# Pairing half slots with full ones in a routed expert layer behind block attention

## The chip, the core and the metric

The kernel runs on one core of a Trainium2 chip. The metric is the device time of one execution in microseconds. Below, PE is TensorE (matmuls and transposes), PEld its weight loads, DVE is VectorE, ACT is ScalarE, POOL is GpSimd and SP is SyncE, which here issues most of the transfers. A line number such as L764 is a line of the kernel before.

## The reference

Attention over 4 batches, 8 heads, 768 positions and 64 dimensions: every query sees the keys less than 16 positions away and one summary key and value for each block of 32 positions (the maximum of the keys, the mean of the values). Its output, 3072 tokens of 512 numbers, goes through a layer of 8 experts of which each token uses one.

```python
k_sum = k.reshape(B, H, nb, block, D).max(axis=3)
v_sum = v.reshape(B, H, nb, block, D).mean(axis=3)
mask_l = np.abs(pos[:, None] - pos[None, :]) < window
scores_s = scale * np.einsum('bhsd,bhnd->bhsn', q, k_sum) + np.log(block)
a = softmax(concatenate([where(mask_l, scores_l, -1e9), scores_s]))
x = matmul(a, concatenate([v, v_sum]))            # then 3072 x 512
e_idx = np.argmax(x @ w_gate, axis=1)
eom = 1.0 / (1.0 + np.exp(-(x @ w_output_gate)))
for e in range(E):
    mask = e_idx == e
    h = np.maximum(x[mask] @ w1[e], 0.0)          # w1: 512 x 1024
    ye = h @ w2[e]                                # w2: 1024 x 512
    out[mask] = gate_w[mask, None] * eom[mask, e, None] * ye
```

With the inputs as drawn, the reference assigns 17, 172, 596, 1384, 768, 0, 135 and 0 tokens to the eight experts; of the first two batches' 1536 tokens, 172, 596 and 768 go to experts 1, 2 and 4.

## The kernel before

**Attention** (`attention`) goes through 48 stages: 4 batches, 6 tiles of 128 positions in each, 2 groups of 4 heads in each tile. A stage makes scores (L321), masks them and takes their minimum on VectorE (L329), exponentiates on ScalarE (L331), transposes (L339), multiplies with the values (L350) and normalises (L358 to L360). Keys and queries are loaded raw, reordered (`reorder`, L205) and transposed (`prep_k`, `prep_q`). `k_sum` copies the block maxima of the keys into the key tile. The block means of the values come from `v_sum`: in batch 0 four sums on VectorE (L230), later adds on GpSimd (L237, L241); `mean` scales them and sends them to DRAM, from where `load_vsum` fetches them into the value windows beside those that `load_vw` brings. The issue order of SyncE in attention is the order in which the code is written; that of the other engines is set by a planner that orders the instructions by its own estimate of times.

**Routing** (`route`) finds each token's expert and its place in the expert's list, and writes token number and gate into the list `l_dr` with one scatter for each tile of 128 tokens (L448, GpSimd). x itself is written to `x_dr` (L363).

**Experts** work in slots. A full slot holds 256 tokens of one expert, a half slot 128. For a slot GpSimd fetches its list (`fetch_list`, L699) and gathers its rows (`fetch`, L712); `take_x` transposes them; `first` makes the hidden layer tile by tile (L763 to L767) and `second` the output (L852 to L854); `write` scales it and scatters it to the output (L872 to L877). Every weight is split into two parts, so each product takes three matmuls, and each tile of raw weights costs a conversion on ScalarE and one on VectorE (L733, L734). `fetch_w` loads the next slot's weights into rings of raw buffers: six before the second pool is open and for w1, ten for w2 after that. While a slot is computed, the rows of the next are transposed at tile 4 of `second`, and the rows of the one after it are gathered.

Slots 0 and 1 are "early": their lists hold tokens of which the list places are known when the routing of the first two batches is done, and slot 0 is started among the last batch's work (`late_work`, `early`). `early_slots` and `rest_slots` compute on VectorE which rows of the lists and which expert each slot has (`slot_tables`). After the early ones come SURE = 6 full slots that are run for any counts, and then, each within a branch on counts that were computed on the chip, more full slots (`more_full`, L903) and then half slots (`more_half`, L910). Each branch is nested in the body of the one before. For the tokens above, 12 full slots and 3 half slots are run. In a half slot the product is made the other way round (L807 to L809) and turned (L820).

The steps of the prediction touch L224 to L247, L293 to L296, L363, L448, L511 to L513, L557, `slot_tables` (L569), `rest_slots` (L633), and in `Experts` `fetch_list`, `fetch`, `first`, `full`, `start`, `early`, `half`, `second`, `write`, `run`, `rest`, `more_full` and `more_half`.

## Time and profile before

| | |
|---|---|
| median of 3 runs | 565.68 us (562.95 to 571.04) |
| the profiled execution | 563.66 us |
| its span, first to last instruction | 561.8 us |
| granted TensorE clock, mean | 0.949 |
| PE busy | 500.7 us (89%) |
| DVE busy | 395.9 us (70%) |
| ACT busy | 339.1 us (60%) |
| POOL busy | 193.1 us (34%) |
| read from HBM, written | 105.50 MB, 13.79 MB |

All times inside the execution count from its first instruction. In the page's slices the span is cut into 40 equal parts of 14 us, and each digit is a busy share in tenths; PEclk is the granted clock in tenths. A row of the timeline gives start, length, engine, line, operation, output and inputs, the count of merged instructions, and in brackets how long the engine had stood idle before it and what ended that. A row of the waits gives who waited for whom, the total, the count and the longest.

### The profile page before, as it was taken

The page shows a single profiled execution, that of the slowest core. Times are in us where ns is not written, and L with a number is a line of the kernel's source. Part 1 is how long each engine was busy: PE and PEld are TensorE (multiplying, and loading weights), DVE is VectorE, ACT ScalarE, POOL GpSimd, SP SyncE. Part 2 cuts the span into 40 slices and gives each one's busy share as a digit, 9 for nine tenths or more (in the row PEclk, how much of TensorE's full clock was granted, in tenths as well). Part 3 has the DMA queues.
Part 4 walks back from the last instruction along what each step waited for, and adds up shares of the span by engine and source line. Part 5 has one row for each costly group of instructions (what it writes and reads, how often), then busy time and mean ns, then how long its engine had stood idle before and what let it go on. Part 6 is the DMA issues. An engine that isn't in the chain of part 4 may idle for free. (4 is left out here: it accounts for less than half of the span.)

```text
span 561.8 us, 12246 instructions
## 1 busy us (share of the span) xinstructions
PE 500.7 (89%) x3880; PEld 436.5 (78%) x3880; DVE 395.9 (70%) x1210; ACT 339.1 (60%) x752; POOL 193.1 (34%) x222
## 2 busy tenths in 40 slices
PE   6498998988979789985999999999999999987990
PEld 5497786767768678874989989899898998975770
DVE  8878798759838857952767665776656666666892
ACT  4386786675749747442656554665555655547881
POOL 6036145445541420337643625415113031130111
PEclk8599998998979979997999999999999999998996
DMA  9979999999764874159667485774856737439790
GB/s 233 232 186 251 235 241 250 115 219 232 163 138 120 247 253 150 65 162 317 211 225 272 151 282 185 236 277 139 300 181 232 269 128 264 168 114 332 252 322 26
DMA packets 116799, 117.63 MB, mean 209 GB/s; under 512 B 53598, under 2 KB 78462, under 8 KB 115952
## 3 DMA queue, kind: packets, MB, share of 16 engines
q1 hardware_dynamic: 107584, 97.02, 61.3%
q0 software_dynamic: 9136, 19.69, 11.5%
q8 instruction: 34, 0.56, 0.5%
q14 instruction: 45, 0.37, 0.2%
HBM read 105.50 MB, written 13.79 MB: 212 GB/s over the span
## 5 line engine op out<-in xcount | busy, mean ns | idle before, releaser
L764 PE MATMUL hp<-xhl,w1h 128*128 128x256 f32 x384 | 109.0, 285 | 0.0
L765 PE MATMUL hp<-xhl,w1l 128*128 128x256 f32 x384 | 108.8, 284 | 0.0
L763 PE MATMUL hp<-xhl,w1h 128*128 128x256 f32 x384 | 108.4, 286 | 0.0
L733 ACT ACTIVATE w2h<-raw 128x512 fp32r<-128x512 f32 x104 | 64.7, 629 | 60.5 <-PE yp L854 27.7
L734 DVE TENSOR_TENSOR w2l<-raw,w2h 128x512 fp32r<-128x512 f32 x104 | 70.5, 689 | 35.2 <-ACT w2h L733 34.2
L852 PE MATMUL yp<-w2h,hh 128*128 128x512 f32 x216 | 87.3, 404 | 0.1
L853 PE MATMUL yp<-w2l,hh 128*128 128x512 f32 x216 | 85.4, 395 | 0.0
L854 PE MATMUL yp<-w2h,hl 128*128 128x512 f32 x216 | 85.2, 396 | 0.1
L331 ACT ACTIVATE pr<-sm,mn 128x120 f32<-128x120 f32 x192 | 62.1, 387 | 26.1 <-DVE mn L329 25.8
L763 PEld LDWEIGHTS hp<-xhl,w1h 128*128 128x128 f32 x384 | 73.7, 193 | 2.0 <-DVE w1l L734 0.4
L712 POOL DMA_INDIRECT xg<-x_dr,lst x28 | 32.3, 1152 | 124.5 <-PE xp L745 106.1
L764 PEld LDWEIGHTS hp<-xhl,w1h 128*128 128x128 f32 x384 | 74.1, 193 | 1.2 <-DVE xhl L748 0.2
L765 PEld LDWEIGHTS hp<-xhl,w1l 128*128 128x128 f32 x384 | 74.1, 193 | 0.0
L766 ACT ACTIVATE hh<-hp 128x256 fp32r<-128x256 f32 x96 | 36.5, 381 | 59.1 <-PE hp L765 57.0
L734 DVE TENSOR_TENSOR w1l<-raw,w1h 128x512 fp32r<-128x512 f32 x104 | 66.2, 690 | 7.3 <-ACT w1h L733 6.2
L767 DVE SCALAR_TENSOR_TENSOR hl<-hp,hh 128x256 fp32r<-128x256 f32 x96 | 39.6, 421 | 44.8 <-ACT hh L766 44.7
L321 PE MATMUL sp<-kt,qt 128*128 128x120 f32 x384 | 58.7, 301 | 7.9 <-DVE kt L296 7.0
L733 ACT ACTIVATE w1h<-raw 128x512 fp32r<-128x512 f32 x104 | 58.2, 621 | 6.9 <-DMA raw<-in_moe_w_dram 6.5
L321 PEld LDWEIGHTS sp<-kt,qt 128*128 128x128 f32 x384 | 53.8, 215 | 10.4 <-issue 8.3
L329 DVE CUSTOM_DVE_ANT_0 sm<-sp,c_sb 128x120 f32<-128x120 f32 x192 | 42.9, 277 | 14.6 <-PE sp L321 13.1
L854 PEld LDWEIGHTS yp<-w2h,hl 128*128 128x128 f32 x216 | 40.7, 189 | 9.5 <-DVE hl L823 0.5
L852 PEld LDWEIGHTS yp<-w2h,hh 128*128 128x128 f32 x216 | 41.2, 191 | 8.6 <-ACT hh L822 0.5
(285 smaller groups left out, 906.5 us busy)
## 6 DMA issues: line engine op xcount, KB each, us to landing
raw<-in_moe_w_dram SPq DMA_DIRECT2D x208, 256.0 KB
vw<-in_v_dram SPq DMA_DIRECT2D x88, 96.0 KB
raw_k<-in_k_dram SPq DMA_DIRECT2D x12, 512.0 KB
raw_q<-in_q_dram SPq DMA_DIRECT2D x12, 512.0 KB
vm<-in_v_dram SPq DMA_DIRECT2D x8, 768.0 KB
x_dr<-xs POOLq DMA_DIRECT2D x24, 256.0 KB, 5.8
vw<-vs_dr SPq DMA_DIRECT2D x36, 48.0 KB
vw<-in_v_dram SPq DMA_DIRECT2D x8, 64.0 KB
```

The lines of the kernel that those rows point to most:

```text
L321: nc.tensor.matmul(sp[:, 2 * x + y, 0:W], lhsT=qt[:, 2 * g + x, li, :], rhs=kt[:, 2 * g + x, blk * KW:blk * KW + W], start=True, stop=True)
L329: nc.vector.tensor_tensor_reduce(out=sm[:, c, :], in0=sp[:, c, 0:W], in1=c_sb[:, m:m + W], scale=1.0, scalar=3.0e38, op0=ALU.add, op1=ALU. ...
L331: nc.scalar.activation(pr[:, c, :], sm[:, c, :], AF.Exp, bias=mn[:, c:c + 1], scale=-1.0)
L733: nc.scalar.activation(hi, raw, AF.Copy)
L734: nc.vector.tensor_tensor(lo, raw, hi.bitcast(F32), ALU.subtract)
L763: nc.tensor.matmul(hp, lhsT=w_h[:, fs], rhs=self.xh[:, c, :], start=c == 0, stop=False)
L764: nc.tensor.matmul(hp, lhsT=w_h[:, fs], rhs=self.xl[:, c, :], start=False, stop=False)
L765: nc.tensor.matmul(hp, lhsT=w_l[:, fs], rhs=self.xh[:, c, :], start=False, stop=c == NC - 1)
L767: nc.vector.scalar_tensor_tensor(hl[:, j, :], hp, 0.0, hh[:, j, :].bitcast(F32), ALU.max, ALU.subtract)
L852: nc.tensor.matmul(y, lhsT=hh[:, j, tk], rhs=w_h, start=j == 0, stop=False)
L853: nc.tensor.matmul(y, lhsT=hh[:, j, tk], rhs=w_l, start=False, stop=False)
L854: nc.tensor.matmul(y, lhsT=hl[:, j, tk], rhs=w_h, start=False, stop=j == NF - 1)
```

## The change

1. Half slots are run in pairs with full ones: `more` runs a full slot and then a half slot in the body of one branch, as often as both are there, and the next pair is nested in it. What is left over, full slots or half slots, stands in the else branch of the pair that is not run, and full and half leftovers are the two arms of a further branch. The last full slots that are left over have a form of their own, `left`: the second product is made for one half of the tokens and written, then for the other half, whose scaling is split over VectorE and ScalarE.
2. The early slots are three, from the lists of the first two batches; "routed" comes in the third batch, and the gather of an early slot is bounded to those two batches' rows. SURE is 5.
3. Scatters of list entries are kept pending. Each write of a tile of x issues two of them; those of the last batch are issued two each behind the ReLU of tiles 1, 4 and 7 of `first` in the next slots. They have a bounds check.
4. Slot 0's weight tiles (8 of w1, 4 of w2) are loaded one by one, three in each of the last batch's tiles 0 to 3, and its list and rows in tiles 1 and 2; before, they came in tiles 3 and 4.
5. The tables of the slots are computed after slot 0's `second` rather than ahead of it, in three parts (sure, pairs, leftovers) beside the early one, and the lists are fetched two a slot.
6. At the start, the sums over v of batch 0 stay on VectorE for four heads only, behind the last copy of `k_sum`; those of the other four heads go to GpSimd, and the means to ScalarE and GpSimd. The reorder of q comes one tile after its load.

```diff
@@ constants
-EARLY = 2
-REST = N - EARLY * SLOT
-SURE = -(-(REST - E * SLOT // 2) // SLOT)
-MOST = (REST + E * (SLOT // 2 - 1)) // SLOT
-NITEM = MOST + 2
+EARLY = 3
+FIRST = 2
+SURE = -(-(N - EARLY * SLOT - E * SLOT // 2) // SLOT)
+MOST = (N + E * (SLOT // 2 - 1)) // SLOT
+PAIRS = max(min((N - h + (E - h) * (SLOT // 2 - 1)) // SLOT - SURE, h) for h in range(E + 1))
+NWOV = SURE + 2 * PAIRS + 2
+NLEFT = max(MOST - SURE, E) + 2
+NITEM = NWOV + NLEFT
@@ body
                     moe.open_first(tc.tile_pool(name="moe1", bufs=2, side="left", reuse_waits="tile"))
+                    moe.start(late_work)
                 elif event == "routed":
                     moe.add_slots(early_slots(tc, const, c_sb, rt))
-                    moe.start(late_work)
                 elif event[0] == "tiles done":
-                    moe.early(event[1])
+                    with tc.manual_schedule(engines={mybir.EngineType.Pool}):
+                        moe.early(event[1])
...
-                slots, halves, counts = rest_slots(tc, const, c_sb, rt)
-            moe.add_slots(slots)
-            moe.fetch_list(EARLY, 2)
-            moe.fetch_w(1, 1, range(NF // 2, NF))
-            moe.second(0, 2, *moe.hidden0, 1, 2, 2)
-            halves = halves()
-            moe.run(halves)
+            moe.fetch_w(1, ("e", 1), range(NF // 2, NF))
+            moe.second(("e", 0), 2, *moe.hidden0, ("e", 1), ("e", 2), 2, 2)
+            counts = rest_slots(tc, const, c_sb, rt, moe)
+            moe.run()
@@ v_sum, mean
-        if b == 0:
+        if (b, o) == (0, 0):
...
+            tc.add_manual_dep(i.ins, km["last"].name, mybir.DependencyInfo(mybir.DependencyClass.NoSync,
+                                                                           mybir.DependencyReason.SCHED_ONLY))
...
-        nc.vector.tensor_scalar(r2, total, 1.0 / 32.0, None, ALU.mult)
+        if b == 0 and o == 0:
+            nc.scalar.activation(r2, total, AF.Copy, scale=1.0 / 32.0)
+        else:
+            (nc.gpsimd if b == 0 else nc.vector).tensor_scalar(r2, total, 1.0 / 32.0, None, ALU.mult)
@@ values
-            nc.gpsimd.dma_start(x_dr[n0:n0 + P, :], xs.rearrange("p h d -> p (h d)"))
+            i = nc.gpsimd.dma_start(x_dr[n0:n0 + P, :], xs.rearrange("p h d -> p (h d)"))
+            scatter(tc, rt, 2, i.ins)
@@ attention, per tile
             if n2 and tt == 0:
                 load("q", q, *n2)
+            elif n2:
                 reorder("q", *n2, RE[5])
...
-        if b == B - 1 and i == n - 2 * TB + 5:
+        if i == n - 2 * TB - 3:
             yield "routed"
+def scatter(tc, rt, n, after, sync=False):
+    for _ in range(min(n, len(rt["pending"]))):
+        i = rt["pending"].pop(0)()
...
+        tc.add_manual_dep(i.ins, after.name, info)
+        rt["scatters"].append(i.ins)
@@ Experts
-            for sc in self.rt["scatters"]:
+            for sc in self.rt["scatters"][:FIRST * TB if s[0] == "e" else None]:
...
-    def full(self, s, nxt, nxt2):
+    def full(self, s, nxt, nxt2, nxt_n=2, lists=()):
         hidden = self.hidden()
         for j in range(NF):
-            self.first(j, hidden, nxt, "S" if j % 2 else "PT")
-        self.second(s, 2, *hidden, nxt, nxt2, 2)
+            i = self.first(j, hidden, nxt, "S" if j % 2 else "PT")
+            if j % 3 == 1:
+                scatter(self.tc, self.rt, 2, i, True)
+        for x in lists[:1]:
+            self.fetch_list(x, 2)
+        self.second(s, 2, *hidden, nxt, nxt2, nxt_n, 2, lists[1:])
+    def left(self, x, lists=()):
...
+        for t in range(2):
+            for j in range(NF):
+                if t == 0 and j == 4:
+                    self.take_x(2)
+                    self.fetch(nxt2, 2)
+                self.second_block(j, yp, hh, hl, [t])
+            self.write(s, yp, [t], t == 1)
@@ start
-        for s in range(EARLY):
-            self.fetch_list(s, 2)
-        self.fetch(0, 2)
-        late_work[3] += [lambda: self.fetch_w(1, 0, range(NF))]
-        late_work[4] += [lambda: self.fetch_w(2, 0, range(NF // 2))]
+        late_work[1] += [lambda: self.fetch_list(("e", 0), 2)]
+        late_work[2] += [lambda: self.fetch(("e", 0), 2)]
+        late_work[3] += [lambda: self.fetch_list(("e", 1), 2)]
+        parts = [(1, i) for i in range(NF)] + [(2, i) for i in range(NF // 2)]
+        for x, (which, i) in enumerate(parts):
+            late_work[x * 4 // len(parts)].append(lambda which=which, i=i: self.fetch_w(which, ("e", 0), [i]))
@@ write
+            if both:
+                h = DM // 2
+                nc.vector.tensor_scalar(y[:, 0:h], yp[t][:, 0:h], lst.bitcast(F32)[:, t, 1:2], None, ALU.mult)
+                nc.scalar.activation(y[:, h:], yp[t][:, h:], AF.Copy, scale=lst.bitcast(F32)[:, t, 1:2])
+            elif t == 0:
@@ in place of the loop over more_full and more_half
+    def more(self, k, n_pairs, n_full, n_half):
+        seen = dict(self.expert)
+        pair = None
+        if k < PAIRS:
+            with self.tc.If(n_pairs > k) as pair:
+                x = SURE + 2 * k
+                lists = [("w", y) for y in range(x + 3, min(x + 5, NWOV))]
+                self.full(("w", x), ("w", x + 1), ("w", x + 2), 1, lists[:1])
+                for y in lists[1:]:
+                    self.fetch_list(y, 2)
+                self.half(("w", x + 1), ("w", x + 2), ("w", x + 3), 2)
+                self.more(k + 1, n_pairs, n_full, n_half)
+            self.expert = dict(seen)
+        with pair.Else() if pair else contextlib.nullcontext():
+            with self.tc.If(n_full > 0) as left:
+                self.left_full(0)
+                self.more_full(1, MOST - SURE - k, n_full)
+            self.expert = dict(seen)
+            with left.Else():
+                self.more_half(0, E - k, n_half)
+        self.expert = seen
```

The slots are named by their kind and place: "e" early, "w" sure and paired, "l" left over.

229 lines of the change are left out of this document (149 added, 80 removed).

## The prediction

> **What bounds the kernel now.** I read the page's slices first, then the busy time by stage, then the order of TensorE's work at the seams between slots, and last the waits and the branches.
>
> ```profile
> PE   6498998988979789985999999999999999987990
> PEclk8599998998979979997999999999999999998996
> GB/s 233 232 186 251 235 241 250 115 219 232 163 138 120 247 253 150 65 162 317 211 225 272 151 282 185 236 277 139 300 181 232 269 128 264 168 114 332 252 322 26
> ```
>
> The busy time by stage:
>
> ```profile
> 150.00:185.00 35.00, 30.34 (x344) 26.54 (x339) 22.11 (x133) 24.46 (x65) 10.28 (x14) 0.90 0.64 149
> 260.00:400.00 140.00, 140.00 (x904) 127.12 (x903) 91.28 (x162) 80.95 (x164) 60.84 (x58) 0.99 0.68 229
> 500.00:562.00 62.00, 42.66 (x187) 31.61 (x185) 40.28 (x64) 37.80 (x66) 9.85 (x8) 0.90 0.66 220
> ```
>
> The windows' columns are length, then busy time of PE, weight load, DVE, ACT and POOL, the granted clock, DMA share and GB/s. From 260 us on the full slots keep TensorE busy for all of the window: there nothing but matmul time counts. TensorE has holes in four other places: the start, the end of attention, slice 18 (near 255 us), and the last 62 us, where it works 42.66 of 62.00. The change touches all four. The seams, from the timeline of TensorE (start, length, then what ended an idle time in brackets):
>
> ```profile
> 232.81 0.38 PE L763 MATMUL hp<-xhl,w1h 128*128 128x256 f32 x1
> ...
> 246.40 0.28 PE L765 MATMUL hp<-xhl,w1l 128*128 128x256 f32 x1
> ...
> 250.64 0.40 PE L854 MATMUL yp<-w2h,hl 128*128 128x512 f32 x1
> 259.38 0.66 PE L745 MATMUL xp<-id_sb,xg 128*128 128x128 f32 x2 [8.33 <-DMA xg<-x_dr,lst]
> ...
> 266.58 0.63 PE L763 MATMUL hp<-xhl,w1h 128*128 128x256 f32 x4
> ...
> 283.56 0.71 PE L745 MATMUL xp<-id_sb,xg 128*128 128x128 f32 x5
> ...
> 290.04 0.28 PE L763 MATMUL hp<-xhl,w1h 128*128 128x256 f32 x1
> ...
> 501.09 0.40 PE L854 MATMUL yp<-w2h,hl 128*128 128x512 f32 x1
> 503.13 0.47 PE L807 MATMUL hp<-w1h,xhl 128*128 128x512 f32 x1 [1.64 <-DVEq L903]
> ...
> 510.55 0.66 PE L820 MATMUL ht<-id_sb,h 128*128 128x128 f32 x4 [3.74 <-ACT h L815]
> ...
> 521.17 0.40 PE L807 MATMUL hp<-w1h,xhl 128*128 128x512 f32 x1
> ...
> 535.26 0.50 PE L807 MATMUL hp<-w1h,xhl 128*128 128x512 f32 x1
> ...
> 548.65 0.40 PE L854 MATMUL yp<-w2h,hl 128*128 128x512 f32 x1
> ```
>
> A full slot takes 290.04 - 266.58 = 23.46 us from first matmul to first matmul. The slot that starts at 232.81 takes 33.77 us, because the gather of the next slot's rows landed 8.33 us late: the excess, 10.31 us, is what that hole costs. The last full slot ends at 501.49 and the last half slot at 549.05: three half slots take 47.56 us, the first 1.64 + 18.04, the second 14.09, the third 13.79. Then 561.8 - 549.05 = 12.75 us pass with no matmul.
>
> **The third early slot.** Today slot 2's list waits for the scatters of the last batch:
>
> ```profile
> 239.81 0.97 POOL L448 DMA_INDIRECT l_dr<-pair,posi  x1 [0.30 <-issue]
> ```
>
> From the end of the last scatter (240.78) to the matmul that needs the gathered rows (259.38) is a chain of 18.6 us: landing, list, gather. After the change slot 2 takes tokens of two batches routed long before, so its list and rows are there and the hole goes: -10.3 us. What is late next? The last six scatters now hang behind the ReLUs of the slot that starts at 232.81, two each at tiles 1, 4 and 7, and the list of "w0", one slot further on, waits for them; behind them on GpSimd's written order stand that list, the gather of w0 and the write of the slot. Tile 7 ends at about 246.7, 13.9 us after the slot's start; with two scatters (0.97 + 0.30 + 0.97, that row's numbers) and a ReLU of some 0.4 the last one is issued by 16.5, and 18.6 us later, at 35.1, w0's rows are there. They are needed at 23.46 + (283.56 - 266.58) = 40.4 us. Slack 5.3 us; I take the whole 10.3, with 5 as the near bound.
>
> **Pairs.** The groups count the slots: 32 matmuls of L763 make a full one, 8 of L807 a half one.
>
> ```profile
> L763 PE MATMUL hp<-xhl,w1h 128*128 128x256 f32 x384 | 108.4, 286 | 0.0
> ...
> L807 PE MATMUL hp<-w1h,xhl 128*128 128x512 f32 x24 | 10.3, 428 | 1.6 <-DVEq L903 1.6
> ```
>
> Twelve full slots and three halves are run today, and by the reference's own token counts the same will be run: experts 2 and 4 hold 596 and 768 tokens after two batches, so three early slots can be filled; then five sure ones, four more full ones, three halves: three pairs and one full slot left for the else branch. The work on TensorE is unchanged; what goes is the seam at 501.49 (the exit from nested branches, which TensorE leaves 1.64 us late on VectorE's side of it, and then 3.74 us behind ACT). A half slot beside a full one has bounds of 11.7 us (half of 23.46) and of 15.9 (47.56 / 3, nothing gained). I take the mean of the two undisturbed ones, 13.94: 47.56 - 41.82 = -5.7 us, range -12 to 0. Cover for the conversions: a pair needs 32 of them on VectorE.
>
> ```profile
> L734 DVE TENSOR_TENSOR w2l<-raw,w2h 128x512 fp32r<-128x512 f32 x104 | 70.5, 689 | 35.2 <-ACT w2h L733 34.2
> ```
>
> From 260 to 400 us VectorE is busy 91.28 of 140.00 us, 15.3 a full slot, of which 16 x 0.689 = 11.0 are conversions. Two slots' worth is 30.6 us, in a pair of 23.46 + 13.94 = 37.4: enough, if the order is right.
>
> **Start.** The sums over v stand in front of the copies that the first scores need:
>
> ```profile
> 15.71 3.64 DVE L230 TENSOR_REDUCE vs<-vm 96x32 f32<-96x1024 f32 x2 [1.30 <-DMA vm<-in_v_dram]
> 19.27 0.30 DVE L296 COPY kt<-km 128x288 f32<-128x288 f32 x1
> ...
> 20.30 3.65 DVE L230 TENSOR_REDUCE vs<-vm 96x32 f32<-96x1024 f32 x2
> ```
> ```profile
> 19.72 2.04 PE L321 MATMUL sp<-kt,qt 128*128 128x120 f32 x8 [4.33 <-DVE kt L296]
> 24.42 0.54 PE L321 MATMUL sp<-kt,qt 128*128 128x120 f32 x1 [2.67 <-DVE kt L296]
> ```
> ```profile
> L241 POOL TENSOR_TENSOR vm<-vm 96x512 f32<-96x512 f32 (+3 forms) x24 | 17.9, 751 | 1.2
> ...
> L237 POOL TENSOR_TENSOR vm<-vm 96x1024 f32<-96x1024 f32 x6 | 14.1, 2356 | 23.0 <-DMA vm<-in_v_dram 22.9
> ```
>
> One pair of sums (3.64) moves behind the copies, the other goes to GpSimd at 2.36 + 4 x 0.75 = 5.4 us. TensorE's two gaps add to 7.0 us, but the sums are needed by the value matmuls, and 5.4 on GpSimd replaces 3.65 on VectorE, so little of it arrives: -2, range 0 to -7.
>
> **Reorder of q one tile later.** Two copies on VectorE stand still on a transfer of q, with everything of VectorE queued behind:
>
> ```profile
> DVE nat_q L211 <- DMA raw_q<-in_q_dram: 6.3, 2, 4.0
> ```
>
> Most of it goes, since a tile later the rows have landed, and prep_q still has two stages in hand: -4, range 0 to -6.3.
>
> **Slot 0's weights over four tiles** rather than two. The end of attention shows TensorE waiting on ACT, which stands in its conversions:
>
> ```profile
> 195.96 0.90 PE L339 MATMUL pt<-id_sb,pr 128*120 128x128 f32 x3 [2.88 <-ACT pr L331]
> ```
>
> Spread, 12 conversions meet a VectorE that is busy 22.11 of 35.00 us: -2, range +3 (they delay scores instead) to -2.9.
>
> **End and tables.** The last slot is now a full one whose two halves of output are written one after the other, the second split over VectorE and ACT:
>
> ```profile
> 549.72 0.74 DVE L872 TENSOR_SCALAR y<-yp,lst_half 128x512 f32<-128x512 f32 x1
> 550.74 1.20 POOL L875 DMA_INDIRECT out_dram<-y,lst_half  x1 [1.36 <-DVE y L872]
> ```
>
> It no longer queues behind a conversion of x (549.05 to 549.72) and is half as long: -1.0. The tables for the slots grow from three to four, some 26 small operations, each between 0.1 and 0.4 us (the row is the largest):
>
> ```profile
> 235.88 0.40 DVE L588 TENSOR_TENSOR pastb<-inc8b,c_sb 128x240 f32<-128x240 f32 x1
> ```
>
> About 5 us more on VectorE over two slots in which it has slack: +1, range 0 to +5. The bounds checks on scatters and the GpSimd mean lie in idle time of GpSimd: nothing; if the cover went, a scatter's 0.97 at most.
>
> **Branches.** A branch that falls through costs nothing one can see; a branch that skips code costs TensorE's sequencer microseconds (min, median, max in ns):
>
> ```profile
> L903 PEldq COMPARE_BRANCH  x6: 65/78/3537, 403.8 to 501.7; - x6
> ...
> L910 PEldq COMPARE_BRANCH  x5: 65/77/4607, 502.4 to 550.7; - x5
> ```
>
> After the change one such jump stands before the left slot (pairs done, into the else branch): TensorE's queue hid all but 1.64 us of the one at 497, so +0.5, range 0 to 4.6. And the exit now has else branches to jump over: +1.5, range 0 to 4.6. The Trainium skill speaks against the change here ("Runtime: NRT & Kernel Launch", Instruction fetch mechanics): a taken branch outside a window of two blocks of code waits for a fetch. The two long branches above agree. By that page each exit that skips an else branch would pay; that is a rival below.
>
> **Sum**, against the profiled execution (563.66 us, of which span 561.8): -10.3 - 5.7 - 2 - 4 - 2 - 1.0 + 1 + 0.5 + 1.5 = -22.0, so 541.7. The median shown, 565.68, lies 2.0 above that execution and the fastest run 0.7 below it, so I stay near the execution and forecast 542, with 533 to 551 as this case's own range.
>
> **Rivals.**
> Loads pace the pairs. A pair moves 32 raw tiles of 256 KB (8.4 MB) and about 1.6 MB of rows in and out: in 37.4 us that is 267 GB/s. The last 62 us moved 220; at that rate a pair takes 45.4, +24 in all; the slices of 332 and 322 GB/s speak against it. Halfway, +12: 554.
> The hole moves to w0: if the chain of 18.6 us grows by more than its 5.3 of slack, up to 10.3 come back: 552.
> Exits in a chain: leaving the left slot and three nested pair bodies, four jumps of 3.5 to 4.6 us in a row, 16 us: 558.
> Slower: SyncE issues in a written order, and from the last batch's tile 0 three weight loads stand in it before the value windows of tiles 3, 4 and 5. From the seventh load on, one waits for a raw buffer that a conversion must free:
>
> ```profile
> SPq L731 <- DVE w1l L734: 137.2, 30, 12.4
> ```
>
> If each of three tiles were held for the longest such wait, 37 us are lost: 579. It decides from 33 us of holding on (22 gained and 11 for 2%). Against it: VectorE's slack in that window, so conversions need not be late by a tile.
> The change doesn't do what it says: a third early slot without tokens costs a whole slot, 23.5 us: 565. The token counts exclude it as far as I see.
>
> **Chances.** Forecast 0.69, loads 0.11, hole moves 0.07, exits 0.07, slower 0.04, not as said 0.02. A measurement here tells about 2% from no change: under 554.4 counts as faster, over 577 as slower. Faster: nearly all of the forecast, half of the loads, most of the moved hole: 0.78. Same: 0.18. Slower: 0.04. The range 531 to 556 leaves out the forecast's low tail, the dearer half of the loads, the exits and the last two.
>
> **What will show it.** No gap before the matmuls of L745 near 250 us, and first matmuls 23.5 us apart from the second early slot on; three pairs of 37.4 us with no gap over 1 us in the half; the first scores before 19 us; no 4 us wait for raw_q; no 2.9 us gap at the last batch's end; 12 to 14 us after the last matmul. It is wrong if the gather of w0 is waited for, if halves take 16 us or more, if the tail exceeds 16 us, or if SyncE's waits move in front of value windows.

## The result and the profile after

| | before | after |
|---|---|---|
| median | 568.36 us (562.95 to 572.15, 4 runs) | 544.1 us (541.73 to 554.24, 4 runs) |
| profiled execution | 563.66 us | 544.58 us |
| its span | 561.8 us | 542.4 us |
| granted TensorE clock, mean | 0.949 | 0.977 |

The ratio is 0.959, with a 95% interval of 0.947 to 0.971: faster. The before column holds one run more than the prediction had. Some executions of a kernel come out longer at a lower granted clock (the one of 554.24 us here had 0.955, and five of eleven of the kernel before in one later set were such), and the ratios leave them out.

The page's slices of the changed kernel, 13.6 us each:

```profile
PE   6688998689978999999989999999999999999990
PEclk8999999999979999999989999999999999999995
```

The hole of slice 18 is gone, and so are the dips near the end: from slice 13 on (counted from 0) TensorE stands at 9 in all slices but slice 20 and the last. The busy time by stage, columns as in the prediction:

```profile
20.00:64.00 44.00, 38.96 (x433) 32.63 (x434) 33.38 (x168) 33.19 (x90) 20.32 (x26) 1.00 0.97 228
64.00:106.00 42.00, 36.25 (x441) 30.80 (x440) 31.95 (x171) 29.11 (x81) 21.72 (x25) 1.00 1.00 218
106.00:150.00 44.00, 39.69 (x457) 33.17 (x457) 36.94 (x217) 32.60 (x89) 21.48 (x26) 1.00 0.97 211
```

The first three windows of the kernel before, for comparison:

```profile
20.00:64.00 44.00, 38.81 (x421) 33.98 (x421) 37.19 (x162) 30.05 (x80) 16.30 (x19) 0.88 0.99 225
64.00:106.00 42.00, 38.82 (x435) 33.32 (x435) 35.05 (x180) 30.41 (x84) 20.98 (x24) 0.96 1.02 211
106.00:150.00 44.00, 38.13 (x430) 32.08 (x426) 35.70 (x197) 30.25 (x83) 19.71 (x23) 0.96 1.01 196
```

The number in brackets after PE's busy time counts matmuls. The changed kernel gets 433, 441 and 457 done where the other got 421, 435 and 430; its DMA engines are as full (0.97 to 1.00) and carry 3 to 15 GB/s more. The seams of the changed kernel, from TensorE's timeline:

```profile
220.23 0.74 PE L845 MATMUL hp<-xhl,w1h 128*128 128x256 f32 x4
...
243.62 0.28 PE L845 MATMUL hp<-xhl,w1h 128*128 128x256 f32 x1
...
262.16 0.98 PE L827 MATMUL xp<-id_sb,xg 128*128 128x128 f32 x7 [0.81 <-DMA xg<-x_dr,lst_w]
...
268.59 0.28 PE L845 MATMUL hp<-xhl,w1h 128*128 128x256 f32 x1
...
389.84 0.28 PE L845 MATMUL hp<-xhl,w1h 128*128 128x256 f32 x1
...
412.87 0.39 PE L919 MATMUL hp<-w1h,xhl 128*128 128x512 f32 x1
...
426.79 0.28 PE L845 MATMUL hp<-xhl,w1h 128*128 128x256 f32 x1
...
450.39 0.39 PE L919 MATMUL hp<-w1h,xhl 128*128 128x512 f32 x1
...
464.91 0.28 PE L845 MATMUL hp<-xhl,w1h 128*128 128x256 f32 x1
...
488.67 0.39 PE L919 MATMUL hp<-w1h,xhl 128*128 128x512 f32 x1
...
503.75 0.36 PE L845 MATMUL hp<-xhl,w1h 128*128 128x256 f32 x1 [1.21 <-ACT w2h L815]
```

L845 opens a full slot and L919 a half one. The pairs begin at 389.84, 426.79 and 464.91 and take 36.95, 38.12 and 38.84 us (the last with the 1.21 us ahead of the left slot). TensorE's last matmul ends at 527.51.

For all that follows the span is cut into three stretches at points that both kernels have: **A**, up to the first matmul of the second early slot (232.81 before, 220.23 after); **B**, seven slots, up to the first matmul of the last four full ones (407.42 before, 389.84 after); **C**, from there to the end, four full slots, three half ones and the tail.

| profiled span, us | A | B | C | of C after the last matmul | span |
|---|---|---|---|---|---|
| before | 232.8 | 174.6 | 154.4 | 12.7 | 561.8 |
| after | 220.2 | 169.6 | 152.6 | 14.9 | 542.4 |
| difference | -12.6 | -5.0 | -1.8 | +2.2 | -19.4 |
| predicted | -8.0 | -9.3 | -4.7 | +0.5 | -22.0 |

The predicted row puts the start, q and the weights into A, the third early slot and the tables into B, and the pairs, the jump, the end and the exit into C. The total is near, the parts are not: A gave half as much again, B about half, C less than half.

### The profile page after: what moved, and what is told of

Same layout as the page of the kernel before. It is cut to its first block, busy times and chain, and to the rows that moved or that the text cites. A ratio compares the mean times of both kernels' runs of the same rounds, so it can differ in the third digit from the quotient of the medians.

```text
span 542.4 us, 12215 instructions
## 1 busy us (share of the span) xinstructions
PE 493.6 (91%) x3880; PEld 428.8 (79%) x3880; DVE 382.4 (71%) x1231; ACT 332.0 (61%) x745; POOL 206.2 (38%) x231
## 3 DMA queue, kind: packets, MB, share of 16 engines
q1 hardware_dynamic: 106432, 94.92, 62.5%
## 4 chain that ended last, share of the span: by engine, by line
PE 56%; DMA 16%; issue 9%; DVE 5%; SPq 3%; POOL 2%; ACT 1%; POOLq 0%; ACTq 0%; DVEq 0%
PE hp L845 7%; PE hp L846 7%; PE hp L847 7%; PE yp L967 7%; PE yp L965 7%; DMA xg<-x_dr,lst_w 7%; PE yp L966 7%; PE sp L338 4%; DMA raw_k<-in_k_dram 3%; DMA raw_q<-in_q_dram 3%; PE pv L367 3%; PE pt L356 2%; PE xp L827 2%; DVE sm L346 1%; DMA vw<-vs_dr 1%
## 5 line engine op out<-in xcount | busy, mean ns | idle before, releaser
L845 PE MATMUL hp<-xhl,w1h 128*128 128x256 f32 x384 | 109.2, 286 | 2.4 <-issue 1.2
L794 POOL DMA_INDIRECT xg<-x_dr,lst_w x26 | 31.3, 1203 | 127.3 <-PE xp L827 120.1
L845 PEld LDWEIGHTS hp<-xhl,w1h 128*128 128x128 f32 x384 | 73.9, 193 | 4.1 <-issue 2.8
L848 ACT ACTIVATE hh<-hp 128x256 fp32r<-128x256 f32 x96 | 35.1, 380 | 57.9 <-PE hp L847 51.7
L338 PE MATMUL sp<-kt,qt 128*128 128x120 f32 x384 | 52.2, 282 | 2.7 <-issue 1.2
L338 PEld LDWEIGHTS sp<-kt,qt 128*128 128x128 f32 x384 | 47.1, 194 | 6.3 <-issue 3.2
L966 PEld LDWEIGHTS yp<-w2l,hh 128*128 128x128 f32 x216 | 40.7, 189 | 7.8
L356 PE MATMUL pt<-id_sb,pr 128*120 128x128 f32 x192 | 38.2, 286 | 7.2 <-ACT pr L348 4.0
L367 PE MATMUL pv<-vw,pT 120*64 120x65 f32 x768 | 36.1, 231 | 5.3 <-DVE xs L377 2.0
L367 PEld LDWEIGHTS pv<-vw,pT 120*64 120x64 f32 x768 | 28.5, 139 | 14.5 <-issue 7.3
```

The costliest lines, as they stand in the source:

```text
L338: nc.tensor.matmul(sp[:, 2 * x + y, 0:W], lhsT=qt[:, 2 * g + x, li, :], rhs=kt[:, 2 * g + x, blk * KW:blk * KW + W], start=True, stop=True)
L356: nc.tensor.transpose(pt[:, c, :], pr[:, c, :], id_sb)
L367: nc.tensor.matmul(po[64 * y:64 * y + 64, 2 * x + hh, :], lhsT=pT[:, 2 * x + y, 64 * hh:64 * hh + 64], rhs=VW[(NB * b + 2 * tok + y) % VR] ...
L845: nc.tensor.matmul(hp, lhsT=w_h[:, fs], rhs=self.xh[:, c, :], start=c == 0, stop=False)
L966: nc.tensor.matmul(y, lhsT=hh[:, j, tk], rhs=w_l, start=False, stop=False)
```

## The experiments

There were four sets, each run beside the kernel before on the same chip (its medians: 559.98, 563.76, 572.02 and 568.81 us), so ratios to it are compared; the shape of the time comes from the profiled execution of each. The changed kernel itself ran in the first set only, and its 0.957 stands for it in the others. A varies by itself: in the first four rows and the fifth, whose attention is the same code, it is 218.9 to 226.1 us. All A, B and C in one table:

| kernel | median us | ratio, 95% interval | A | B | C |
|---|---|---|---|---|---|
| the changed kernel, again | 536.26 | 0.957 (0.950 to 0.964) | 218.9 | 164.8 | 150.8 |
| not paired, nested branches | 544.84 | 0.973 (0.966 to 0.980) | 220.6 | 167.1 | 153.6 |
| pairs, no branches | 547.3 | 0.975 (0.968 to 0.982) | 221.3 | 182.0 | 143.3 |
| not paired, no branches | 548.5 | 0.976 (0.969 to 0.983) | 226.1 | 178.4 | 144.2 |
| pairs, no branches, order kept | 532.88 | 0.937 (0.929 to 0.945) | 221.8 | 164.9 | 143.7 |
| q's reorder as before | 536.36 | 0.953 (0.947 to 0.960) | 217.6 | 164.8 | 150.5 |
| start as before | 539.44 | 0.958 (0.953 to 0.963) | 223.5 | 164.8 | 152.2 |
| weights in two tiles, as before | 540.76 | 0.961 (0.955 to 0.967) | 222.3 | 164.8 | 153.1 |
| two early slots | 548.9 | 0.973 (0.967 to 0.979) | 223.0 | 172.5 | 153.0 |
| scatters in bursts, three batches | 550.46 | 0.966 (0.958 to 0.974) | 232.2 | 164.7 | 154.0 |
| scatters in bursts, two batches | 553.51 | 0.969 (0.962 to 0.976) | 233.9 | 165.5 | 153.5 |
| q as before, last scatters early | 544.05 | 0.956 (0.950 to 0.963) | 217.4 | 168.3 | 153.8 |

**The changed kernel again.**

> The changed kernel once more, as the yardstick of this set. Its profile had a third early slot of 24.97 us and a first sure slot of 27.30 us where the others take 23.49. If the gather of the first sure slot is late by construction and code fetch is the rest, both come back within 1 us of that; if they were chance, both go to about 23.5.

It took 536.26 us where the kernel before took 559.98 in the same set. B was 164.8 us, 9.8 below the kernel before, of the 10.3 at which the hole was priced. The 169.6 of the first profile held two things that did not come again, the wait of 0.81 us for w0's gather and a slot w0 of 27.30 us (23.50 here). In it TensorE stood three times with no wait that the profile shows (0.28, 0.44 and 0.79 us, less than half of the 3.8 us); the longest:

```profile
278.12 0.28 PE L845 MATMUL hp<-xhl,w1h 128*128 128x256 f32 x1 [0.79 <-issue]
```

**Pairs against branches.** Three kernels: full slots and then halves in nested branches, as before; pairs with no branches; neither pairs nor branches. All three suit these inputs only: the two without branches have their counts written in, and the nested one the place of its first half slot.

```diff
-    nc.vector.tensor_tensor(pairs, full, half, ALU.min)
+    nc.vector.tensor_scalar(pairs, half, 0.0, None, ALU.mult)
...
-        self.more(0, n_pairs, n_full, n_half)
+        self.plain_full(0, n_full)
+        self.plain_half(0, n_half)
...
```

> The changed kernel, but the four further full slots and then the three half slots stand in nested branches one after the other, as in the kernel before (where the first half starts is written in for these inputs). Seam theory (what was slow was the exit from the nested branches): the first half again takes about 18 us after a gap near 1.6, the other two 14, so the slots cost 5.7 us more, the exit at the end some 2 less: 3 to 6 us over the changed kernel. Pairing theory (halves side by side starve for loads): all three halves over 15.5 us.

```diff
-        self.more(0, n_pairs, n_full, n_half)
+        for k in range(3):
+            x = SURE + 2 * k
...
+            self.full(("w", x), ("w", x + 1), ("w", x + 2), 1, lists[:1])
...
+            self.half(("w", x + 1), ("w", x + 2), ("w", x + 3), 2)
+        self.left_full(0)
```

> The three pairs and the left slot with no branches at all (the counts of these inputs are written in). Branch costs by the changed kernel's rows: 1.21 us of idle TensorE before the left slot and about 2.5 us on GpSimd at the end. Seam theory: 3.7 us under the changed kernel, tail near 12.5. If branches also keep the planner from mixing slots, 6 us or more under it.

```diff
-    nc.vector.tensor_tensor(pairs, full, half, ALU.min)
+    nc.vector.tensor_scalar(pairs, half, 0.0, None, ALU.mult)
...
-        self.more(0, n_pairs, n_full, n_half)
+        for x in range(SURE, SURE + 4):
+            self.full(("w", x), ("w", x + 1), ("w", x + 2), lists=[("w", x + 3)])
+        for x in range(SURE + 4, SURE + 7):
+            self.fetch_list(("w", x + 3), 2)
+            self.half(("w", x), ("w", x + 1), ("w", x + 2), 1, True)
```

> Four full slots, then three half slots, no branches (the counts of these inputs are written in). Seam theory: pairing itself gives nothing, so this comes within 1.5 us of the pairs without branches, halves 13.5 to 14.5 us each. Pairing theory: halves side by side are held by loads and conversions, 15.5 us or more each, 5 us over the pairs without branches.

With the nested branches the old seam is back, first its jump on TensorE's sequencer, then the two waits on its timeline:

```profile
L1022 PEldq COMPARE_BRANCH  x6: 65/78/3557, 384.1 to 482.0; - x6
```
```profile
485.87 0.47 PE L919 MATMUL hp<-w1h,xhl 128*128 128x512 f32 x1 [4.01 <-DVEq L1022]
...
492.80 0.66 PE L932 MATMUL ht<-id_sb,h 128*128 128x128 f32 x4 [1.67 <-ACT h L927]
```

From the first of the last four full slots to the last matmul this kernel takes 142.0 us (387.67 to 529.66), the changed one 136.0 (383.63 to 519.67): the seam costs 5.95 us. Its tail is 3.2 us shorter, so C differs by only 2.8 us. The two profiled spans differ by 6.8 us; the other 4.0 stand in A and B, where only the choice of the lists fetched ahead was changed, and are not shown to be the pairs'. Without branches the same work takes 135.2 us in pairs and 134.3 unpaired: side by side, a half slot gains nothing from a full one. What the pairs gain is that TensorE no longer crosses a jump between full slots and halves.

Both kernels without branches were slower than the changed one all the same (the 3.7 us gain forecast for the first missed), in B. In the one with pairs GpSimd made twelve list fetches for later slots (two a slot) ahead of the rows that were due next. Its timeline, with the first of them and the gather behind them, and then TensorE's two longest waits:

```profile
251.64 0.95 POOL L781 DMA_INDIRECT lst_w<-l_dr,rowic  x1 [0.30 <-DVE hl L849]
...
269.12 1.25 POOL L794 DMA_INDIRECT xg<-x_dr,lst_w  x1 [0.30 <-issue]
```
```profile
272.88 0.66 PE L827 MATMUL xp<-id_sb,xg 128*128 128x128 f32 x2 [4.79 <-DMA xg<-x_dr,lst_w]
...
288.44 0.45 PE L827 MATMUL xp<-id_sb,xg 128*128 128x128 f32 x1 [6.08 <-DMA xg<-x_dr,lst_w]
```

From 251.64 to 269.12 GpSimd does nothing but list fetches, twelve in 17.5 us. In the changed kernel those fetches stand in the branch bodies and do not move ahead; the next run tests whether their order is the cause.

**No branches, the order kept.** The same kernel, with the last seven slots under the written order of GpSimd:

```diff
             moe.run()
-        moe.rest(counts)
+            moe.rest(counts)
```

> The kernel without branches, with the counts of these inputs written in, once more, now with the fetches of lists and the gathers of the last seven slots kept in the order in which they are written. In the first such kernel twelve fetches of later lists stood ahead of the gather for the fourth slot (252 to 268 us, 1.26 us each) and cost 13.4 us of waits. No part of the computation is left out for these inputs, but other counts of tokens would not be computed. Theory: what the branches cost is then the difference to the changed kernel: 6.7 us of its end (14.75 for 8.08) and about 1 us at the jump, so 528 to 529 us where the changed kernel has 536.3, ratio 0.943. Rival: the branches cost nothing that the straight code does not pay in another place (loads of instructions, later gathers), ratio 0.955 or more.

B is 164.9 us, as in the changed kernel: the order was the cause. The ratio is 0.937, below the forecast 0.943 though its interval holds that; the 528 to 529 us were missed. The kernel with branches in the same set (the last of the table) has 0.956, but it also lost 3.5 us in B, so the gap of 2% overstates the branches. By the profiles C is 7.1 us shorter than in the changed kernel, 1.3%, and 6.7 of it lie after the last matmul (8.09 us for 14.75). So branches are dear here, and at the end rather than at the jumps between the pairs. The sequencers' rows of the changed kernel (its second profile) at the branch that leads out, L1045, with count, shortest, median and longest in ns and the first and last start; then those of the end, L1082:

```profile
L1045 POOLq EVENT_SEMAPHORE  x4: 17/43/2596, 521.2 to 524.0; - x4
...
L1045 PEldq COMPARE_BRANCH  x2: 3293/3695/4097, 515.3 to 519.9; - x2
...
L1045 POOLq COMPARE_BRANCH  x2: 38/48/58, 520.7 to 525.5; - x2
...
L1045 POOLq INC_SWDGE_SEM  x1: 1397/1397/1397, 524.1 to 524.1; - x1
```
```profile
L1082 POOLq DRAIN  x3: 103/180/5060, 528.0 to 534.0; - x3
```

GpSimd issues the last scatter of results, and then, before it may leave the branch, waits 2.60 us for it to land and spends 1.40 us on its queue's semaphores. It branches at 525.5, is at the end's code at 528.0, 2.5 us later, and only then starts its drain of 5.06 us. TensorE's jump of 4.10 us lies beside this. The kernel before left its last branch with the same steps (L910, then its end, L936):

```profile
L910 POOLq COMPARE_BRANCH  x5: 34/38/50, 509.1 to 556.1; - x5
L910 POOLq EVENT_SEMAPHORE  x4: 17/43/43, 550.7 to 554.7; - x4
L910 POOLq INC_SWDGE_SEM  x1: 1303/1303/1303, 554.7 to 554.7; - x1
...
L936 POOLq DRAIN  x3: 46/103/4726, 556.2 to 561.5; - x3
```

Its last scatter starts at 550.74, and GpSimd sees it landed at 554.7, too; then come 1.30 us for the semaphores, the branch at 556.1 and the drain at 556.2. So the landing and the semaphores are not new in the changed kernel. The 2.5 us between branch and drain are: there they are 0.15, and in the kernel with nested branches 0.16, which is most of why its tail is 3.2 us shorter. The kernel without branches:

```profile
L1086 POOLq DRAIN  x3: 46/103/6203, 523.3 to 530.1; - x3
```

Its drain of 6.20 us begins at 523.3, before the last scatter has even started (523.55), and covers the landing. The Trainium skill ("Perfetto Trace Analysis", DMA Instruction — SWDGE (GPSIMD)) says that such a row ends when the descriptors are written, not when the data has moved; the trace agrees: the last scatter's row starts at 520.98 and takes 0.98 us, and GpSimd waits for the landing until 524.0.

**The parts of A, undone one at a time.** First q: a tile of q is put in order (`reorder`) in the step that loads it. The expectation calls this a sixth piece; in the code `RE[5]` only names the engine, and the whole tile is reordered at once.

```diff
             if n2 and tt == 0:
                 load("q", q, *n2)
-            elif n2:
                 reorder("q", *n2, RE[5])
```

> The changed kernel with one part undone: the sixth piece of a query tile is put in order in the tile that loads it, as in the kernel before. No work is left out. The prediction's step: this piece is why the sort of the query tile stood in the matmuls' path twice (2.37 and 3.98 us), so the undo gives those waits back and costs about 4 us: ratio to the kernel before 0.964 where the changed kernel has 0.957. Rival, from the profile after (waits of this kind summing to about 14 us where they were 6 us): the move only shifted the waits or made them longer, so the undo costs nothing or gains up to 4 us: ratio 0.950 to 0.958, and fewer of the waits in the groups.

0.953 against 0.957: no loss, if anything a gain, and the rival holds. VectorE's waits for q, in the kernel before, the changed one (first profile), this one, and the one with the start undone (the next experiment), which keeps the later place:

```profile
DVE nat_q L211 <- DMA raw_q<-in_q_dram: 6.3, 2, 4.0
```
```profile
DVE nat_q L220 <- DMA raw_q<-in_q_dram: 14.5, 7, 4.4
```
```profile
DVE nat_q L220 <- DMA raw_q<-in_q_dram: 9.9, 5, 4.2
```
```profile
DVE nat_q L220 <- DMA raw_q<-in_q_dram: 4.5, 4, 3.6
```

The waits grew with the change, but not by the later place: they are 4.5 us with it when the start is undone, and 12.9 us without it in the last kernel of the table. With the new start they are 9.9 to 16.1 us in every kernel but the two with bursts (8.1 and 4.6), which come through attention later. A reading that fits, and that no run tests: the DMA engines are full throughout the first three batches (the windows above), so q lands when the queue lets it, and where attention gets there sooner, it waits longer.

The start, with all of batch 0's sums and means on VectorE and no order behind the copies:

```diff
-        if (b, o) == (0, 0):
+        if b == 0:
...
-            tc.add_manual_dep(i.ins, km["last"].name, ...)
...
```

> The changed kernel with one part undone: the sums and means of batch 0 all stand on VectorE, and no order holds the sum behind the copies of the means of k, as in the kernel before. No work is left out. The prediction's step: first scores back from 16.3 to about 19.7 us, end later by about 2 us (ratio 0.961 for 0.957), granted clock of the first batch as it was in the changed kernel (1.00). Rival: the start also sets how the clock is granted in the first three batches (before: 0.88, 0.96, 0.96; after: 1.00 each), in which case the last values product of the third batch falls back from 146.6 to 150 us or later, and the end is 5 to 6 us later (ratio 0.967).

The first scores went back from 16.26 to 19.07 us, and in the profile, one execution, the third batch ended at 150.3 us as the rival had it (147.3 in the changed kernel's second profile) and A is 4.6 us longer. The ratio of the timed runs is 0.958 all the same: against 0.957, nothing that can be resolved, and the 4.6 us lie within what A varies by itself. The granted clock was 0.89 and 0.88 in the first two windows, but that is not the start's doing by this evidence: with the start left as changed, the first window has 0.88 in the kernel with two early slots and 0.92 in the pairs without branches. The first batch ended at 62.5 us regardless (62.3 at 1.00), the second at 108.6 (103.8 at 0.94); whether the clock or the order of work made the second late isn't settled.

The weights of slot 0, asked for in the tiles 3 and 4:

```diff
-        for x, (which, i) in enumerate(parts):
-            late_work[x * 4 // len(parts)].append(lambda ...: self.fetch_w(which, ("e", 0), [i]))
+        late_work[3] += [lambda: self.fetch_w(1, ("e", 0), range(NF))]
+        late_work[4] += [lambda: self.fetch_w(2, ("e", 0), range(NF // 2))]
```

> The changed kernel with one part undone: slot 0's second and third weights are asked for in tiles 3 and 4 of the last batch, as in the kernel before, and not over tiles 0 to 3. No work is left out. The prediction's step: 2 us later (ratio 0.961), with waits of the last batch's matmuls in the tiles 3 to 5. Rival, from the last batch's 50.2 us after where it took 56.6 us before: the spread is worth more, 4 to 6 us (ratio 0.964 to 0.968). Second rival: it is worth nothing, because the last batch became shorter by its routing and its clock alone (ratio 0.957).

0.961: the predicted ratio, though the intervals of the two overlap. A wait behind ACT is back near the end of the last batch, and slot 0 takes 33.15 us where it took 28.92:

```profile
184.60 0.47 PE L356 MATMUL pt<-id_sb,pr 128*120 128x128 f32 x1 [2.56 <-ACT pr L348]
```

Two early slots, with the tables ahead of slot 0's second product, as before. The last batch's six scatters then stand in one burst ahead of it, too:

```diff
-EARLY = 3
+EARLY = 2
...
-            moe.second(("e", 0), 2, *moe.hidden0, ("e", 1), ("e", 2), 2, 2)
-            counts = rest_slots(tc, const, c_sb, rt, moe)
...
+            counts = rest_slots(tc, const, c_sb, rt, moe)
...
+            moe.fetch_list(("w", 0), 2)
+            moe.second(("e", 0), 2, *moe.hidden0, ("e", 1), ("w", 0), 2, 2)
```

> The changed kernel with two early slots in place of three: the first two batches' lists give two slots, the tables of the others are made ahead of the second half of slot 0, and the slot that follows is fetched after them. The work is the same, one slot has moved from the early kind to the others. The prediction's step: the hole before the third slot comes back, about 10.3 us, so the second slot takes 33 to 34 us where the changed kernel has 23.4, less the 3 to 5 us that the third early slot spends above 23.5: ratio 0.970 to 0.976. Rival (the hole moves along with the tables, whatever the count of early slots): the third slot's delay is already paid in the changed kernel, and the time is the same within 2 us (ratio 0.954 to 0.961).

The hole is back in the same place, and B is 7.7 us longer:

```profile
248.62 0.66 PE L834 MATMUL xp<-id_sb,xg 128*128 128x128 f32 x2 [6.05 <-DMA xg<-x_dr,lst_w]
```

The ratio, 0.973, is what the prediction's step gives; the rival, a hole that merely moves, is out.

**What was left of A: the scatters.** The list entries of a batch are scattered in one burst when the batch is routed, not two behind each store of x.

```diff
             rt["pending"].append(lambda t=t: nc.gpsimd.indirect_dma_start(...))
+        while b < B - 1 and rt["pending"]:
+            i = rt["pending"].pop(0)()
...
```

> The changed kernel with one part undone: the list entries of the first three batches are scattered in one burst of six when a batch is routed, as in the kernel before, and not two at a time behind each store of x. No work is left out. Undoing the pairs, the third early slot, the spread of the weights, the start and the order of the query tile one at a time gave 1.6, 1.6, 0.4, 0.1 and -0.4 per cent, 3.3 of the 4.3 that the change gains. Theory: the rest lies in the bursts (each holds GpSimd for about 7.7 us in the path of the sums of v and the stores of x), so this run is 3 to 6 us later, ratio 0.962 to 0.968, and the third and fourth batches are longer. Rival: bursts and pairs of scatters cost the same, because GpSimd is idle for half of these batches, ratio 0.957 within 2 us.

A is 13.3 us longer in the profile, and the ratio 0.966. In the same set the highest of six times of the table's last kernel, which has no such bursts in attention, is 546.48 us, and the lowest of four with bursts 548.81. One window of 10 us as an example; TensorE's clock was 1.00 in both, six scatters stand in a row in the burst, from 136.92 to 144.52, and the changed kernel has four in that window, two and two. The changed kernel (its second profile), and then the kernel with bursts:

```profile
135.00:145.00 10.00, 9.92 (x124) 7.83 (x122) 9.11 (x67) 7.95 (x22) 5.48 (x7) 1.00 0.68 159
```
```profile
135.00:145.00 10.00, 7.33 (x77) 5.61 (x76) 5.76 (x42) 3.61 (x12) 7.09 (x8) 1.00 0.55 137
```

All engines but GpSimd do less; three stops of TensorE with no wait shown (1.08, 0.53 and 0.46 us) make 2.1 of the 2.7 us in which it stands idle. With bursts SyncE stands up to 9.4 us at a load of value windows until TensorE has come far enough to free the buffer. The changed kernel's longest such wait here is 3.1, that of any kernel without bursts 5.4 at most, that of the kernel before, which has bursts, 12.1. What stands behind that load in the written order, slot 0's weights among it, comes later; that the delay is handed on this way fits these rows, but no run isolates it. SyncE's rows of the waits (total, times, longest), again the changed kernel and then the other:

```profile
SPq L271 <- PE pt L356: 7.6, 7, 3.1
```
```profile
SPq L271 <- PE pt L356: 14.9, 6, 9.4
```

In the third batch's burst TensorE can be seen to stand. These are its value matmuls and the last three scatters, with other rows left out:

```profile
195.54 0.51 PE L367 MATMUL pv<-vw,pT 120*64 120x65 f32 x9
196.00 0.97 POOL L466 DMA_INDIRECT l_dr<-pair,posi  x1 [0.30 <-issue]
196.44 0.35 PE L367 MATMUL pv<-vw,pT 120*64 120x65 f32 x4 [0.39 <-issue]
197.28 0.97 POOL L466 DMA_INDIRECT l_dr<-pair,posi  x1 [0.30 <-issue]
197.91 0.29 PE L367 MATMUL pv<-vw,pT 120*64 120x65 f32 x2 [1.12 <-issue]
198.55 0.97 POOL L466 DMA_INDIRECT l_dr<-pair,posi  x1 [0.30 <-issue]
199.35 0.22 PE L367 MATMUL pv<-vw,pT 120*64 120x65 f32 x1 [1.16 <-issue]
```

Sixteen matmuls that elsewhere run in 0.69 us take 4 us, in steps of about 1.45, and wait for nothing that the profile shows. The burst as such does not do this: in the kernel before, scatters stand six in a row four times, and TensorE's rows show no idle time of over 0.15 us without a releaser; six in a row in the kernel with two early slots (223.18 to 230.55) have none beside them either. And with two at a time such stops occur, as in the changed kernel's first profile, behind its two scatters at 88.7 and 90.1:

```profile
91.50 0.33 PE L356 MATMUL pt<-id_sb,pr 128*120 128x128 f32 x1 [1.30 <-issue]
```

To place the loss, the third batch's scatters alone went back to two behind each store:

```diff
-        while b < B - 1 and rt["pending"]:
+        while b < B - 2 and rt["pending"]:
```

> The kernel with bursts once more, but the third batch's six scatters, which fell into the last batch's work at 192 to 200 us, go two behind each store of x again; the bursts of the first two batches stay. No work is left out. With all three bursts the third and fourth batches took 49.1 and 52.9 us (changed kernel: 43.5 and 48.2) and the slot that runs into the last batch 32.7 (28.9). Theory, each burst stops the matmuls where it stands: the last batch falls back to about 48 us and that slot to 28.9, the third batch stays near 49, and about half of the loss goes: ratio 0.961 to 0.963. Rival, the loss is not the burst's but comes with the third batch's later lists and weights: both batches stay as long, ratio 0.965 or more. Second rival, it is the run's order of work as a whole that was bad by chance: no pattern by batch.

0.969: the loss stayed, and the first theory's halves did not come. The third batch took 50.7 us and the fourth 54.2 (43.5 and 48.2 in the changed kernel). The third alone tells little, as it took 48.1 and 51.2 us in two of the kernels without branches, whose attention is as in the changed kernel; the fourth took 45.1 to 50.6 us in every kernel without bursts. So the bursts of the first two batches are enough for the loss, and the second one's delay may reach the last batch through SyncE's order (longest wait 11.4 us here). The test was not clean for the third burst, as two of its stores came together, four scatters stood in a row (194.13 to 199.02), and TensorE stood for 1.1 us at a time there again.

**The last scatters earlier,** with q's reorder as before:

```diff
...
-            if j % 3 == 1:
+            if j < 3:
                 scatter(self.tc, self.rt, 2, i, True)
```

> The changed kernel with two edits: the sixth piece of a query tile in the tile that loads it, as in the kernel before, and the last six scatters behind the hidden tiles 0, 1 and 2 of the second early slot where they stood behind 1, 4 and 7. No work is left out. Theory: the list of the first slot of the second kind is fetched about 8 us sooner (239 where it was 247 to 249), its gather is in 5 us before it is needed, so the wait of 0.8 us that one profile showed cannot come back; the median itself gains at most 1 us on the run with the query piece alone: ratio 0.950 to 0.955. Rival: the wait on the last scatter's landing is not the gather's limit, the tables on VectorE are (the list's row index ends at 246 to 248), and the list is no earlier: ratio as with the query piece alone, 0.953.

0.956, the same as the changed kernel within the interval. The list came 6 to 8 us earlier, at 241.28, where VectorE's tables held it (as in the changed kernel's second profile, by its row), and the gather ended at 249.6: no wait for w0 any more, but none was paid in the changed kernel's second profile either. B was 3.5 us longer instead (slots of 24.78 and 26.12 us). Of these, 2.5 us are stops of TensorE without a wait shown, the longest behind six scatters that now stood in a row up to 231.92:

```profile
233.22 0.28 PE L845 MATMUL hp<-xhl,w1h 128*128 128x256 f32 x1 [1.04 <-issue]
```

So nothing is won here, and q's reorder in its old place isn't confirmed as a gain either.

## Why the prediction was right, and where not

The forecast of 542 us was close to the measured 544.1, through errors that cancel.

- **The third early slot** (-10.3, and +1 for the tables) held: B fell by 9.8 us in the second profile, and two early slots cost 1.6% (9 us). The slack of 5.3 us for w0 did not: it was -0.8 in the first profile and about nothing in the second. So one of the prediction's signs of being wrong, that the gather of w0 is waited for, did show once. The chain was to start when the last scatter ends, 16.5 us into the slot; that was 21.0, with slower scatters (1.42 and 1.95 us instead of 0.97), and the list started only at 248.93. Its row names VectorE, in the second profile the last table's rows (`rowid`, L648), which in both profiles end 0.2 to 1.1 us before the list. So the tables, moved behind slot 0's second product, seem to pace the list; the prediction gave them a price on VectorE and no place in this chain:

```profile
239.26 1.95 POOL L466 DMA_INDIRECT l_dr<-pair,posi  x1 [0.30 <-issue]
248.93 0.99 POOL L781 DMA_INDIRECT lst_w<-l_dr,rowib  x1 [7.71 <-DVE hl L849]
...
255.91 1.01 POOL L794 DMA_INDIRECT xg<-x_dr,lst_w  x1 [2.80 <-PE yp L967]
```

- **The pairs** (-5.7): the seam was read rightly and cost 5.95 us when it was put back; halves took 13.92, 14.52 and 13.87 us (15.08 less the gap of 1.21), for 13.94 predicted. That the half slot is covered by the full one had no part in it, as the runs without branches show. Over all of C the nested branches cost only 2.8 us more, since their end is 3.2 us shorter.
- **The jump into the else branch** (+0.5): 1.21 and 0.76 us. Right in kind, a little short.
- **End and exit** (-1.0 and +1.5): the end held, the exit was mis-sized. The tail grew by 2.2 us, not 0.5, and came out at 14.9 where 12 to 14 were foretold. From the last matmul to the last scatter's landing the changed kernel takes 4.4 us (527.51 to 531.9) where the other took 5.6, so -1.2. The exit makes up the rest, +3.4, of which 2.5 are GpSimd's jump from its last branch to its drain, 2.6 us for 0.15. The prediction priced the jump by TensorE's sequencer, where it is off the path; it counts on GpSimd, which must also see its last scatter landed before it may leave. Landing (2.60), semaphores (1.40) and jump (2.5) come to 6.5 of the 6.7 us by which the tail stands above that of the kernel without branches. The rival of exits in a chain is refuted: TensorE's sequencer made two far jumps at L1045 in the first profile, one of 3.29 us under the last matmuls and one of 4.26 us behind them, not four in a row. What the Trainium skill says of taken branches ("Runtime: NRT & Kernel Launch", Instruction fetch mechanics), that a target outside the fetched window has to be fetched first, agrees with far jumps of 3.29 to 4.26 us on TensorE's sequencer and with the 0.07 to 0.08 us of branches not taken. That GpSimd's 2.5 us are such a fetch is shown by no row, and the wait on the transfer is not in that rule.
- **q one tile later** (-4): wrong. The waits went from 6.3 us to 14.5, and the sign "no 4 us wait for raw_q" failed with one of 4.4. The step took the place of the reorder for the cause; but the later place has 4.5 us with the old start, and undoing the place lost nothing. Why q lands late was not tested.
- **Slot 0's weights** (-2): 0.4% as a ratio, 2.4 us, held as far as it can be resolved; the gap of 2.88 us is gone (the longest wait behind ACT's `pr` in the last batch is 1.15).
- **The start** (-2): not resolved (0.1%).
- **Missing from the sum: the scatters.** The prediction priced their bounds check and their place behind the last batch, and not that spreading them over the stores of x takes bursts out of attention. That is worth about 1%, 5 to 7 us, by two kernels whose intervals overlap that of the changed one at their ends (0.966 and 0.969 for 0.957), and would be most of what A gained beyond the forecast. That the bursts cost is shown by these runs; the way in which they do is argued.
- **The rivals**: loads did not pace the pairs (38.84 us at most, and in the first profile no gap of over 0.5 us on TensorE but the 1.21 at the jump); the hole did not move to w0, but for the 0.81 us; SyncE's order did not turn it slower.

The undone parts add up to 1.6 + 1.6 + 0.4 + 0.1 - 0.4 + 0.9 = 4.2% of the 4.3%. That the sum closes is partly luck, as each term has an interval of about 0.7%, most come from another set than the changed kernel's, and of the pairs' 1.6% only a third was found in the stretch that was changed.

What stays open: why TensorE stands for up to 1.3 us at a time with no releaser shown. After the first scores, stops of over 0.25 us occur five to twelve times each in the changed kernel's first profile (six) and in all four kernels of the last two sets, whether they have bursts or not, and at most once in the kernel before and in the eight kernels of the first two sets. So they seem to go with the set a kernel ran in; long rows of scatters or list fetches are not shown to be their cause.

## What to carry to other kernels

In this kernel the branches cost most where the last one is left: ask what transfer the engine that ends last must see landed before it may jump, and how far that engine's own jump is, and compare with a copy that has the counts written in. Moving the consumer of a load later in the code does not bring the load sooner; before pricing such a step, ask what sets the time of its landing. When a change also re-places small operations of a side engine, such as the scatters here, price their bursts too. And before a stop is put down to what stands beside it, look for the same neighbour in the kernel before.

## What the runs showed of the hardware

- Leaving the last branch with a transfer of GpSimd in flight cost 2.60 us for its landing, 1.40 us for the queue's semaphores and 2.5 us for the jump, one after the other. In the kernel before landing and semaphores were there too, and the jump took 0.15 us. Straight code hid the first two in a drain of 6.20 us.
- Code without the branches let twelve list fetches in 17.5 us run ahead of due gathers and lost 17.2 and 13.6 us in B; with their written order kept, nothing was lost there.
- Matmuls stood for up to 1.3 us at a time with no wait shown (once 16 matmuls in 4 us instead of 0.69) beside rows of scatters, but also where two scatters stood alone; four rows of six in the kernel before had none of it.
- The mean granted clock was 0.977 in the changed kernel and 0.949 before, in the first three windows 1.00 for 0.88, 0.96 and 0.96. In kernels with the new start the first window ranged from 0.88 to 1.00, so how much of A's gain is the clock's own can't be told from these runs; with the start undone it was 0.89, and the first batch ended 0.2 us later.
